# Pre-split first weights kept in DRAM, pairwise sums of the attention weights, and moved steps, in an attention, MLP and expert-MLP kernel

## The chip, the cores and the metric

One core of a Trainium2 chip runs the whole kernel in one launch. The metric is device time in microseconds, median of several runs; lower is better. Engines: PE (TensorE), ACT (ScalarE), DVE (VectorE), POOL (GpSimd), and SP (SyncE), whose queue issues nearly all DMAs.

## The reference

```python
# q, k, v: (4, 12, 448, 64) float32; g_q, g_k: (64,)
q_n, k_n = rmsnorm(q, g_q), rmsnorm(k, g_k)
attn = softmax(q_n @ k_n.T / sqrt(64))          # sum + 1e-9 below the line
x = (attn @ v) laid out as (1792, 768)
h = x @ w_in                                    # (768, 2048), float64 in DRAM
x = (h * clip(h + 3, 0, 6) / 6) @ w_out         # (2048, 768), float64 in DRAM
# then: logits = x @ w_gate (8 experts); greedy assignment by descending logit,
# 224 tokens an expert; out = relu(x @ w1[e]) @ w2[e]
```

All else is float32. The two float64 weights come in as int64 bits.

## The kernel before

Products that must be near float32 are done in fp32r with each operand split in two: a rounded high part `h` (ACT) and a low part `l` = raw - h (DVE or POOL), and three products hh, hl, lh. Attention goes over 24 pairs of heads. One pair takes 16 steps of a schedule of events written out by hand: `at(t, fn, ...)` with t = 16 i + an offset (the T_ constants), sorted by t, gives one program order, which each engine and SP's queue then keep. Pair i's maxima (`s1`, L301/L304, `mt`/`mr` L310/L312) come before its transposed scores (`sT`, L323), the exponentials (L334) and the product with v (`pv`, L413). For 17 of 24 pairs the result stays transposed (head dim by tokens); the other seven (`QMAJOR`: batch 0 and the last pair) go over `av`, `normalize`, `xt`.

For the 17 pairs the sums of the exponentials are made so: POOL adds the four key blocks of each head, three additions in a row (`padd`, L406); PE multiplies with ones (`psums`, L421) and ACT copies it (L423); SP writes two rows to DRAM and reads them back spread over 112 partitions (`rs_out` L427, `rs_in` L432); DVE adds 1e-9 (L436) and inverts (L437); SP writes that out and reads it as a broadcast (`r_out` L441, `r_in` L447); POOL multiplies (`xmul` L452), and ACT and DVE split the result (L460, L461).

Between the steps a queue of atoms is drained by `fill`: the first product of the batch before (`mlp1_atoms`, L499), 16 units of 18 products a batch, for batches 0 to 2. A unit loads its 384 KB of w_in (`win_load`, L174), splits it (`win_split`, ACT L114; DVE or POOL by turns, L115), and ends with the gate (ACT L502, DVE L504) and the store of g (SP, L505). Batch 2 also carries `wprime_atoms`, which fold the router's weights into w_out. Batch 3 follows after attention. The float64 weights are turned into float32 by `conv` and `narrow`: 16 units of 128 columns of w_in from step 20, one every 10 steps, and 16 of w_out from step 180, one every 12; four DVE steps (L137 to L140) on following schedule steps, and a store (L165, L167). All SBUF tiles and the eight PSUM buffers (one ring, tag "b") have a fixed number of buffers.

After attention come batch 3's first product, the second product with the routing between (L1103), and the experts (L1187, L1251); w_out and the experts' weights are loaded and split as units too (`wout_unit`, `moe_unit`).

Of the kernel before, what the change touches and what calls it, by code (L numbers as in the profile page):

```python
# [21 lines left out]
def kernel(  # L22
# [28 lines left out]
    VB, CB = 6, 1  # L51
# [24 lines left out]
    T_ADD, T_PV, T_SUM = (6, 12.5, 14), (17, 17.1, 19.5, 19.6), 21  # L76
    T_RS, T_RL, T_REC, T_RO, T_RB, T_X, T_XS = 24, 26, 30, 31.5, 33, 37, 38.5
# [56 lines left out]
    def narrow(lo, hi, v):  # L134

        vi = v.bitcast(I32)
        return (lambda: nc.vector.tensor_scalar(v, hi.bitcast(F32), 2.0 ** -112, None, op0=OP.mult),  # L137
                lambda: nc.vector.tensor_scalar(vi, vi, 3, None, op0=OP.logical_shift_left),
                lambda: nc.vector.scalar_tensor_tensor(vi, lo, 29, vi, op0=OP.logical_shift_right, op1=OP.bitwise_or),
                lambda: nc.vector.scalar_tensor_tensor(vi, hi, -2147483648, vi, op0=OP.bitwise_and, op1=OP.bitwise_or))  # L140

    RAW = {}

    def conv(key, part):
# [16 lines left out]
        v32, steps = RAW[key]  # L161
        steps[part]()
        if part == 3:
            if out_:
                nc.sync.dma_start(wo32[rows, :], v32)  # L165
            else:
                nc.sync.dma_start(w32[:, rows].rearrange("(c p) f -> p c f", p=128), v32.rearrange("p (c f) -> p c f", c=NC))  # L167
# [9 lines left out]
    def win_split(u, v32):  # L177
        h = wpool.tile([128, NC, 128], F32R, name="wh", tag="w", bufs=WB)
        l = wpool.tile([128, NC, 128], F32R, name="wl", tag="w", bufs=WB)
        split(v32, h, l, nc.vector if u % 2 else nc.gpsimd)  # L180
        return h, l
# [157 lines left out]
    def av(i, s, n):  # L339
# [26 lines left out]
        if (s, n) == (0, QT - 1):  # L366
            NUM[i] = (apool.tile([CP, NCH, 2, D], F32, name="num", bufs=1), apool.tile([CP, 2, NCH], F32, name="scol", bufs=1),
                      apool.tile([CP, NCH, 2, D], F32, name="xq", bufs=1))
# [31 lines left out]
    PA, PV, RC = {}, {}, {}  # L400

    def padd(i, n):
        for s in range(2):
            if n == 1:
                PA[i, s] = apool.tile([CP, S], F32, name="pa", bufs=2)
            nc.gpsimd.tensor_tensor(PA[i, s], PA[i, s] if n > 1 else PP[i, s, 0][0], PP[i, s, n][0], op=OP.add)  # L406
# [11 lines left out]
    def psums(i):  # L418
        p = ps.tile([128, 512], F32, name="sm", tag="b", bufs=8)
        for s, r in enumerate(ROWS):  # L420
            nc.tensor.matmul(p[r, :S], ones64, PA.pop((i, s)), start=True, stop=True)  # L421
        RC[i] = apool.tile([128, S], F32, name="sms", bufs=1)
        nc.scalar.activation(RC[i], p[:, :S], AF.Copy)  # L423

    def rs_out(i):
        d = dram.tile([2, S], F32, name=f"sum_dr{i}")
        nc.sync.dma_start(d, RC[i][0:128:64, :])  # L427
        RC[i] = d
# [6 lines left out]
    def rec(i):  # L435
        nc.vector.tensor_scalar(RC[i], RC[i], eps[:CP], None, op0=OP.add)  # L436
        nc.vector.reciprocal(RC[i], RC[i])  # L437
# [6 lines left out]
    def r_in(i):  # L444
        t = apool.tile([128, S], F32, name="rb", bufs=1)
        for s, r in enumerate(ROWS):
            nc.sync.dma_start(t[r, :], RC[i][s:s + 1, :].to_broadcast([64, S]))  # L447
        RC[i] = t

    def xmul(i):  # L450
        n = PV[i]
        nc.gpsimd.tensor_tensor(n, n, RC.pop(i), op=OP.mult)  # L452

    def xsplit(i):
        b, j = divmod(i, NP)
        if j == 0:
            XT[b] = [xpools[b % 2].tile([128, NC, S], F32R, name=n) for n in ("xh", "xl")]
        xh, xl = XT[b]
        n = PV.pop(i)
        nc.scalar.activation(xh[:, j], n, AF.Copy)  # L460
        nc.vector.tensor_tensor(xl[:, j], n, xh[:, j].bitcast(F32), op=OP.subtract)  # L461
# [4 lines left out]
    units_in = list(range(NF)) * B  # L466
    GB = 2

    def prefetch(splits=2):

        while len(ready) < splits and loaded:
# [4 lines left out]
    def mlp1_atoms(b, inline):  # L476
# [13 lines left out]
        def mm(f, n):  # L490
# [9 lines left out]
            if n == 3 * NC - 1:  # L500
# [4 lines left out]
                nc.sync.dma_start(g_dr[b][f * 128:(f + 1) * 128, :], g)  # L505
                if inline:
                    gsplit(b, f, g, nc.vector)

        for f in range(NF):
            for n in range(3 * NC):  # L510
                atoms.append(lambda f=f, n=n: mm(f, n))
                if inline and n == 10 and f > 1:
                    atoms.append(lambda f=f: lg(b, f - 2))
        if inline:
# [188 lines left out]
    for i in range(NH // 2):  # L703
# [24 lines left out]
        else:  # L728
            for n in range(1, NCH):
                at(t + T_ADD[n - 1], padd, i, n)  # L730
            for d, fn in ((T_SUM, psums), (T_RS, rs_out), (T_RL, rs_in), (T_REC, rec), (T_RO, r_out), (T_RB, r_in), (T_X, xmul), (T_XS, xsplit)):
                at(t + d, fn, i)
        if (i + 1) % NP == 0:
# [4 lines left out]
    for u in range(NF if wide else 0):  # L738
        for out_, t in ((0, T_CI + D_CI * u), (1, T_CO + D_CO * u)):
            at(t - T_CL, conv, (out_, u), -1)  # L740
            for part in range(4):
                at(t + part, conv, (out_, u), part)
# [310 lines left out]
    def moe_tile(name):  # L1053
        k = nw[0] % (WB + EB)
        nw[0] += 1
        if k < WB:
            return wpool.tile([128, 768], F32R, name=name, tag="w", bufs=WB)
        return big_tile(name)

    def moe_unit(e, j, eng, after=None):  # L1060
# [10 lines left out]
        h, l = moe_tile("weh"), moe_tile("wel")  # L1071
# [227 lines left out]
```

## Time and profile before

| what | value |
|---|---|
| median of 3 runs | 1279.39 us (1275.06 to 1279.78) |
| the profiled execution's own time | 1273.12 us |
| its span | 1271.3 us |
| mean granted TensorE clock | 0.962 |
| PE / PEld busy | 1160.6 / 929.6 us |
| DVE / ACT / POOL busy | 861.0 / 549.2 / 559.2 us |
| DMA | 205.68 MB, 162 GB/s |

Times are us from the span's start. PEld is PE's weight load. In a row, `out<-in` names the tiles, x gives the count; "idle before" is time in which the engine stood still just before such an instruction, and `<-` what ended it. The granted clock is the mean over a stretch, as a part of 2.4 GHz. A busy matmul's end is modelled.

### The profile page before, as it was taken

How to read it: one execution, taken by the hardware profiler on the slowest of the kernel's cores; microseconds unless marked ns; L12 is line 12 of the kernel's file. 1: busy time of each engine (PE TensorE's matmuls, PEld its weight loads, DVE VectorE, ACT ScalarE, POOL GpSimd, SP SyncE). 2: the span in 40 equal slices, each digit the busy share in tenths (PEclk: the TensorE clock that was granted, in tenths of full speed). 3: DMA queues.
4: the chain of work that ended last, by engine and by line, in shares of the span. 5: the costliest groups of instructions: out<-in, count | busy, mean ns of one | idle time of the engine just before them, and what ended most of it. 6: DMA issues, size and time to landing. Idle time of an engine off the chain costs nothing.

```text
span 1271.3 us, 19668 instructions
## 1 busy us (share of the span) xinstructions
PE 1160.6 (91%) x7136; PEld 929.6 (73%) x7136; DVE 861.0 (68%) x1662; ACT 549.2 (43%) x1019; POOL 559.2 (44%) x395
## 2 busy tenths in 40 slices
PE   4988798889998998899998999999999799999997
PEld 2877456565655666568776777777777799999997
DVE  7988967878887985444687366666667566655550
ACT  3544454444543544454675311111112565566650
POOL 2212755665766564122344222222224476666641
PEclk9988898999998999999998999999999899999999
DMA  4456666465655555434998422222224888777731
GB/s 126 142 158 182 179 169 178 150 197 156 190 176 168 166 175 165 142 105 127 311 303 269 126 72 63 75 63 76 63 76 108 221 247 246 236 238 235 227 122 44
DMA packets 228885, 205.68 MB, mean 162 GB/s; under 512 B 24082, under 2 KB 208052, under 8 KB 228788
## 3 DMA queue, kind: packets, MB, share of 16 engines
q1 hardware_dynamic: 225460, 193.42, 51.5%
q0 software_dynamic: 3328, 11.01, 2.9%
q8 instruction: 56, 0.92, 0.3%
q14 instruction: 41, 0.34, 0.1%
HBM read 165.99 MB, written 38.39 MB: 161 GB/s over the span
## 4 chain that ended last, share of the span: by engine, by line
PE 38%; DVE 6%; issue 4%; DMA 3%; ACT 1%; POOL 1%; POOLq 0%; DVEq 0%; ACTq 0%
PE y L1103 16%; PE y L1251 8%; PE h L1187 5%; PE h L499 2%; PE h L1189 2%; PE rt L914 2%; DMA we_s<-in_moe_w_dram 1%; DVE C L909 1%; DMA gr<-g_dr 1%; DVE gl L529 1%; PE lg L542 1%; PE lg L541 1%; PE xp L1135 1%; DVE wel L115 1%; ACT weh L114 0%
## 5 line engine op out<-in xcount | busy, mean ns | idle before, releaser
L1047 POOL TENSOR_TENSOR g2l<-gr,g2h 128x512 fp32r<-128x512 f32 x60 | 78.8, 1316 | 210.1 <-ACT g2h L1045 162.8
L499 PE MATMUL h<-xh,wh 128*128 128x448 f32 x384 | 157.3, 410 | 8.6 <-DVE mr L312 4.2
L499 PE MATMUL h<-xl,wh 128*128 128x448 f32 x384 | 147.6, 384 | 0.0
L499 PE MATMUL h<-xh,wl 128*128 128x448 f32 x384 | 147.3, 384 | 0.0
L115 POOL TENSOR_TENSOR wel<-we_s,weh 128x768 fp32r<-128x768 f32 x60 | 119.3, 1994 | 63.2 <-ACT weh L114 52.9
L115 DVE TENSOR_TENSOR wel<-we_s,weh 128x768 fp32r<-128x768 f32 x68 | 93.7, 1385 | 71.4 <-ACT weh L114 71.2
L114 ACT ACTIVATE weh<-we_s 128x768 fp32r<-128x768 f32 x128 | 105.4, 841 | 63.7 <-DMA we_s<-in_moe_w_dram 48.0
L1103 PE MATMUL y<-woh,g2l 128*128 128x512 f32 (+1 forms) x448 | 128.7, 349 | 1.0 <-POOL g2l L1047 1.0
L1187 PE MATMUL h<-xe,weh 128*128 128x448 f32 x384 | 124.6, 385 | 5.3 <-DVE xe L1138 5.3
L1045 ACT ACTIVATE g2h<-gr 128x512 fp32r<-128x512 f32 x60 | 37.7, 631 | 209.3 <-PE y L1103 156.6
L1103 PE MATMUL y<-woh,g2h 128*128 128x512 f32 (+1 forms) x448 | 128.1, 349 | 0.0
L1103 PE MATMUL y<-wol,g2h 128*128 128x512 f32 (+1 forms) x448 | 126.6, 346 | 0.0
L499 PEld LDWEIGHTS h<-xh,wh 128*128 128x128 f32 x384 | 76.0, 198 | 50.9 <-issue 29.7
L334 ACT ACTIVATE ph<-st 112x448 f32<-112x448 f32 x192 | 92.1, 543 | 45.3 <-PE st L323 44.4
L304 DVE TENSOR_REDUCE mx<-s 112x1 f32<-112x448 f32 x192 | 107.0, 611 | 1.3 <-PE s L301 1.2
L115 POOL TENSOR_TENSOR wl<-win_v,wh 128x768 fp32r<-128x768 f32 x32 | 64.0, 2002 | 97.9 <-ACT wh L114 95.8
L406 POOL TENSOR_TENSOR pa<-pa,ph 112x448 f32<-112x448 f32 x68 | 94.4, 1415 | 0.4 <-ACT ph L334 0.4
L1189 PE MATMUL h<-xe,wel 128*128 128x224 f32 x384 | 94.6, 273 | 0.0
L1251 PE MATMUL y<-weh,hl 128*112 128x384 f32 x256 | 86.4, 338 | 0.0
L1251 PE MATMUL y<-weh,hh 128*112 128x384 f32 x256 | 86.3, 337 | 0.0
L1251 PE MATMUL y<-wel,hh 128*112 128x384 f32 x256 | 86.3, 337 | 0.0
L499 PEld LDWEIGHTS h<-xh,wl 128*128 128x128 f32 x384 | 76.1, 198 | 12.5 <-issue 4.1
(249 smaller groups left out, 2664.0 us busy)
## 6 DMA issues: line engine op xcount, KB each, us to landing
we_s<-in_moe_w_dram SPq DMA_DIRECT2D x128, 384.0 KB, 4.5
win_v<-w SPq DMA_DIRECT2D x64, 384.0 KB, 5.0
g_dr<-g SPq DMA_DIRECT2D x64, 224.0 KB, 2.6
gr<-g_dr SPq DMA_DIRECT2D x52, 256.0 KB, 2.9
wraw<-in_moe_w_in_dram SPq DMA_DIRECT2D x16, 768.0 KB, 7.2
wraw<-in_moe_w_out_dram SPq DMA_DIRECT2D x16, 768.0 KB, 6.1
gr<-g_dr SPq DMA_DIRECT2D x48, 224.0 KB, 5.4
w<-cv SPq DMA_DIRECT2D x16, 384.0 KB, 3.1
```

The source lines that it names most:

```text
L114: nc.scalar.activation(hi, raw, AF.Copy)
L115: eng.tensor_tensor(lo, raw, hi.bitcast(F32), op=OP.subtract)
L304: mx = nc.vector.tensor_reduce(MX[i][:, s, c:c + 1], pp[s][:CP, :S], axis=AX.X, op=OP.max)
L334: nc.scalar.activation(e, pp[s][:CP, :S], AF.Exp)
L406: nc.gpsimd.tensor_tensor(PA[i, s], PA[i, s] if n > 1 else PP[i, s, 0][0], PP[i, s, n][0], op=OP.add)
L499: nc.tensor.matmul(p[:, :S], w[:, c], x[:, c], start=(n == 0), stop=(n == 3 * NC - 1))
L1045: nc.scalar.activation(gh, g, AF.Copy)
L1047: eng.tensor_tensor(gl, g, gh.bitcast(F32), op=OP.subtract)
L1103: nc.tensor.matmul(pp[hf][:, :COLS[hf].stop - COLS[hf].start], a[:, f % QF], w[:, COLS[hf]], start=(f == 0 and n == 0), stop=(f == NF - 1 ...
L1187: mm = [lambda: nc.tensor.matmul(p[:, :4 * CP], wh[:, fo], x.rearrange("d k t -> d (k t)"), start=(c == 0), stop=(c == NC - 1), skip_group ...
L1189: lambda: nc.tensor.matmul(p[:, :2 * CP], wl[:, fo], x[:, 0], start=False, stop=False, skip_group_check=True)]
L1251: nc.tensor.matmul(p[:CP, :HW], a[:, f, tk], w[:, o], start=(f == 0 and n == 0), stop=(f == FB - 1 and n == 2))
```

## The change

In `conv`, a unit of w_in is also split right after its conversion (ACT, then POOL), and both parts go to a DRAM tensor `w_hl`. The first 48 units of the first product (batches 0 to 2) load that pair ready made, 768 KB in one transfer (`win_whole`); the last 16 still load float32 and split. The first narrowing step runs on ACT; the store of the converted unit is one step later. `padd` makes two independent additions a head, and `psums` adds their results on PE, four products. The 1e-9 is added by ACT's copy, into the buffer `rb` that then takes the broadcast as well. The places of the chain of the sums move ahead, and `xsplit`'s low part goes to POOL. g is stored six products into the next unit. `normalize` works in place; the stage buffers `v` go from 6 to 4; high and low weight tiles share one buffer each pair.

```diff
     NF = FF // 128
     NTC = NT // 128
     NSL = NT // CP
-    VB, CB = 6, 1
+    VB, CB = 4, 1
     WB = 6
     OB = 3
     PB = 12
...
     T_ST = (0, 0.1, 8, 8.1)
     T_AV = ((17, 18, 19.5, 20.5), (22, 23, 24.5, 25.5))
     T_NUM, T_XT, T_MLP = 28, 33, (37, 41, 41, 37)
-    T_ADD, T_PV, T_SUM = (6, 12.5, 14), (17, 17.1, 19.5, 19.6), 21
-    T_RS, T_RL, T_REC, T_RO, T_RB, T_X, T_XS = 24, 26, 30, 31.5, 33, 37, 38.5
+    T_ADD, T_PV, T_SUM = (6, 14), (17, 17.1, 19.5, 19.6), 21
+    T_RS, T_RL, T_REC, T_RO, T_RB, T_X, T_XH, T_XL = 22.5, 24.5, 27.5, 28.5, 30.5, 35, 36, 37.5
+    GD = 6
     QMAJOR = tuple(range(NP)) + (B * NP - 1,)
     T_CI, D_CI, T_CO, D_CO, T_CL = 20, 10, 180, 12, 14
...
     def narrow(lo, hi, v):
         vi = v.bitcast(I32)
-        return (lambda: nc.vector.tensor_scalar(v, hi.bitcast(F32), 2.0 ** -112, None, op0=OP.mult),
+        return (lambda: nc.scalar.activation(v, hi.bitcast(F32), AF.Copy, scale=2.0 ** -112),
                 lambda: nc.vector.tensor_scalar(vi, vi, 3, None, op0=OP.logical_shift_left),
                 lambda: nc.vector.scalar_tensor_tensor(vi, lo, 29, vi, op0=OP.logical_shift_right, op1=OP.bitwise_or),
                 lambda: nc.vector.scalar_tensor_tensor(vi, hi, -2147483648, vi, op0=OP.bitwise_and, op1=OP.bitwise_or))
     RAW = {}
+    wide_b = range(B - 1) if wide else ()
+    w_hl = [dram.tile([128, 2, 768], F32, name=f"w_hl{u}") for u in range(NF if wide else 0)]
     def conv(key, part):
...
             raw = RAW[key]
             v32 = rawp.tile([128, 768], F32, name="cv", bufs=CB)
             RAW[key] = (v32, narrow(raw[:, :, 0], raw[:, :, 1], v32))
-        v32, steps = RAW[key]
-        steps[part]()
-        if part == 3:
+        v32, steps = RAW[key][:2]
+        if part < 4:
+            steps[part]()
+        elif part == 5:
+            hl = rawp.tile([128, 2, 768], F32R, name="whl", bufs=1)
+            RAW[key] += (hl,)
+            nc.scalar.activation(hl[:, 0], v32, AF.Copy)
+        elif part == 6:
+            hl = RAW[key][2]
+            nc.gpsimd.tensor_tensor(hl[:, 1], v32, hl[:, 0].bitcast(F32), op=OP.subtract)
+        elif part == 8:
+            nc.sync.dma_start(w_hl[n], RAW[key][2].bitcast(F32))
+        elif part == 4:
             if out_:
                 nc.sync.dma_start(wo32[rows, :], v32)
             else:
...
         return u, v32
     def win_split(u, v32):
-        h = wpool.tile([128, NC, 128], F32R, name="wh", tag="w", bufs=WB)
-        l = wpool.tile([128, NC, 128], F32R, name="wl", tag="w", bufs=WB)
-        split(v32, h, l, nc.vector if u % 2 else nc.gpsimd)
-        return h, l
+        w = wpool.tile([128, 2, NC, 128], F32R, name="w", bufs=WB // 2)
+        split(v32, w[:, 0], w[:, 1], nc.vector if u % 2 else nc.gpsimd)
+        return w[:, 0], w[:, 1]
+
+    def win_whole(u):
+        w = wpool.tile([128, 2, NC, 128], F32R, name="w", bufs=WB // 2)
+        nc.sync.dma_start(w.rearrange("p a c f -> p a (c f)").bitcast(F32), w_hl[u])
+        return w[:, 0], w[:, 1]
     a_stack = ExitStack()
...
         if n % QT < QT - 1:
             return
         if (s, n) == (0, QT - 1):
-            NUM[i] = (apool.tile([CP, NCH, 2, D], F32, name="num", bufs=1), apool.tile([CP, 2, NCH], F32, name="scol", bufs=1),
-                      apool.tile([CP, NCH, 2, D], F32, name="xq", bufs=1))
+            NUM[i] = (apool.tile([CP, NCH, 2, D], F32, name="num", bufs=1), apool.tile([CP, 2, NCH], F32, name="scol", bufs=1))
+            NUM[i] += (NUM[i][0],)
         num, sc, _ = NUM[i]
         m = slice(n - QT + 1, n + 1)
         pv = p[:CP, :QT * W].rearrange("p (n w) -> p n w", w=W)
...
         nc.vector.tensor_tensor(xl[:, j], t[:, :S], xh[:, j].bitcast(F32), op=OP.subtract)
-    PA, PV, RC = {}, {}, {}
+    PA, PV, RC, RB = {}, {}, {}, {}
     def padd(i, n):
         for s in range(2):
-            if n == 1:
-                PA[i, s] = apool.tile([CP, S], F32, name="pa", bufs=2)
-            nc.gpsimd.tensor_tensor(PA[i, s], PA[i, s] if n > 1 else PP[i, s, 0][0], PP[i, s, n][0], op=OP.add)
+            PA[i, s, n] = apool.tile([CP, S], F32, name="pa", bufs=4)
+            nc.gpsimd.tensor_tensor(PA[i, s, n], PP[i, s, 2 * n][0], PP[i, s, 2 * n + 1][0], op=OP.add)
     def pv(i, c):
         if c == 0:
...
     def psums(i):
         p = ps.tile([128, 512], F32, name="sm", tag="b", bufs=8)
-        for s, r in enumerate(ROWS):
-            nc.tensor.matmul(p[r, :S], ones64, PA.pop((i, s)), start=True, stop=True)
-        RC[i] = apool.tile([128, S], F32, name="sms", bufs=1)
-        nc.scalar.activation(RC[i], p[:, :S], AF.Copy)
+        for n in range(2):
+            for s, r in enumerate(ROWS):
+                nc.tensor.matmul(p[r, :S], ones64, PA.pop((i, s, n)), start=(n == 0), stop=(n == 1))
+        RB[i] = apool.tile([128, S], F32, name="rb", bufs=1)
+        nc.scalar.activation(RB[i], p[:, :S], AF.Identity, bias=eps)
     def rs_out(i):
         d = dram.tile([2, S], F32, name=f"sum_dr{i}")
-        nc.sync.dma_start(d, RC[i][0:128:64, :])
+        nc.sync.dma_start(d, RB[i][0:128:64, :])
         RC[i] = d
     def rs_in(i):
...
         RC[i] = t
     def rec(i):
-        nc.vector.tensor_scalar(RC[i], RC[i], eps[:CP], None, op0=OP.add)
         nc.vector.reciprocal(RC[i], RC[i])
     def r_out(i):
...
         RC[i] = d
     def r_in(i):
-        t = apool.tile([128, S], F32, name="rb", bufs=1)
+        d = RC.pop(i)
         for s, r in enumerate(ROWS):
-            nc.sync.dma_start(t[r, :], RC[i][s:s + 1, :].to_broadcast([64, S]))
-        RC[i] = t
+            nc.sync.dma_start(RB[i][r, :], d[s:s + 1, :].to_broadcast([64, S]))
     def xmul(i):
         n = PV[i]
-        nc.gpsimd.tensor_tensor(n, n, RC.pop(i), op=OP.mult)
-
-    def xsplit(i):
+        nc.gpsimd.tensor_tensor(n, n, RB.pop(i), op=OP.mult)
+
+    def xsplit(i, lo):
         b, j = divmod(i, NP)
-        if j == 0:
+        if not lo and j == 0:
             XT[b] = [xpools[b % 2].tile([128, NC, S], F32R, name=n) for n in ("xh", "xl")]
         xh, xl = XT[b]
-        n = PV.pop(i)
-        nc.scalar.activation(xh[:, j], n, AF.Copy)
-        nc.vector.tensor_tensor(xl[:, j], n, xh[:, j].bitcast(F32), op=OP.subtract)
+        if lo:
+            nc.gpsimd.tensor_tensor(xl[:, j], PV.pop(i), xh[:, j].bitcast(F32), op=OP.subtract)
+        else:
+            nc.scalar.activation(xh[:, j], PV[i], AF.Copy)
     lgp = {}
     late, tpool, ready, loaded = [], [], [], []
     units_in = list(range(NF)) * B
+    whole = [len(wide_b) * NF]
     GB = 2
     def prefetch(splits=2):
+        while whole[0] and len(ready) < splits:
+            ready.append(win_whole(units_in.pop(0)))
+            whole[0] -= 1
+        if whole[0]:
+            return
         while len(ready) < splits and loaded:
             ready.append(win_split(*loaded.pop(0)))
         while units_in and len(loaded) < 3 and (len(units_in) > NF or len(loaded) + len(ready) < 3 or tpool):
...
                 nc.scalar.activation(r, p[:, :S], AF.Relu, bias=half, scale=1.0 / 6.0)
                 g = mpool.tile([128, S], F32, name="g", bufs=GB)
                 nc.vector.scalar_tensor_tensor(g, r, 1.0, p[:, :S], op0=OP.min, op1=OP.mult)
-                nc.sync.dma_start(g_dr[b][f * 128:(f + 1) * 128, :], g)
+                state["g", f] = g
                 if inline:
                     gsplit(b, f, g, nc.vector)
+
+        def g_out(f):
+            nc.sync.dma_start(g_dr[b][f * 128:(f + 1) * 128, :], state.pop(("g", f)))
         for f in range(NF):
             for n in range(3 * NC):
                 atoms.append(lambda f=f, n=n: mm(f, n))
+                if n == GD and f > 0:
+                    atoms.append(lambda f=f: g_out(f - 1))
                 if inline and n == 10 and f > 1:
                     atoms.append(lambda f=f: lg(b, f - 2))
+        atoms.append(lambda: g_out(NF - 1))
         if inline:
             for f in (NF - 2, NF - 1):
                 late.append(lambda f=f: lg(b, f))
...
             at(t + T_NUM, normalize, i)
             at(t + T_XT, xt, i)
         else:
-            for n in range(1, NCH):
-                at(t + T_ADD[n - 1], padd, i, n)
-            for d, fn in ((T_SUM, psums), (T_RS, rs_out), (T_RL, rs_in), (T_REC, rec), (T_RO, r_out), (T_RB, r_in), (T_X, xmul), (T_XS, xsplit)):
+            for n in range(2):
+                at(t + T_ADD[n], padd, i, n)
+            for d, fn in ((T_SUM, psums), (T_RS, rs_out), (T_RL, rs_in), (T_REC, rec), (T_RO, r_out), (T_RB, r_in), (T_X, xmul)):
                 at(t + d, fn, i)
+            at(t + T_XH, xsplit, i, False)
+            at(t + T_XL, xsplit, i, True)
         if (i + 1) % NP == 0:
             at(t + T_MLP[i // NP], mlp_next, i // NP)
     at(T_LOAD, load_scales)
...
     for u in range(NF if wide else 0):
         for out_, t in ((0, T_CI + D_CI * u), (1, T_CO + D_CO * u)):
             at(t - T_CL, conv, (out_, u), -1)
-            for part in range(4):
-                at(t + part, conv, (out_, u), part)
+            for part in range(5 if out_ else 9):
+                if part != 7:
+                    at(t + part, conv, (out_, u), part)
     events.sort(key=lambda e: e[:2])
     ENDS = [8 * H * (b + 1) - 16 + T_MLP[b] for b in range(B)]
     now = 0
...
```

## Rows read from the trace of the kernel before

**Rows 1.** Windows: stretch, length, busy PE, PEld, DVE, ACT, POOL; clock, DMA share, GB/s

```profile
50.00:150.00 100.00, 84.08 (x667) 68.36 (x664) 88.98 (x170) 49.22 (x100) 34.43 (x28) 0.91 0.67 182
150.00:300.00 150.00, 132.45 (x692) 87.23 (x690) 120.43 (x186) 71.00 (x128) 87.44 (x61) 0.94 0.58 170
300.00:450.00 150.00, 137.98 (x725) 93.61 (x726) 126.59 (x195) 71.40 (x131) 92.25 (x63) 0.94 0.57 177
450.00:570.00 120.00, 106.42 (x601) 72.59 (x600) 64.09 (x113) 54.08 (x120) 47.69 (x36) 0.94 0.47 145
570.00:690.00 120.00, 110.29 (x584) 89.33 (x583) 86.63 (x124) 74.94 (x137) 46.20 (x29) 0.97 0.83 257
```

**Rows 2.** Waits of PE, 150 to 570: us in total, times, longest

```profile
PE t L278 <- DVE mx L304: 6.2, 2, 3.5
...
PE s L301 <- DVE g L504: 0.4, 1, 0.4
```

**Rows 3.** Lines: busy us, mean ns, idle before and its releasers

```profile
L115 DVE TENSOR_TENSOR wl<-win_v,wh 128x768 fp32r<-128x768 f32 x32 | 40.2, 1255 | 3.4 <-ACT wh L114 2.0 <-PE lg L541 1.0
...
L115 POOL TENSOR_TENSOR wl<-win_v,wh 128x768 fp32r<-128x768 f32 x32 | 64.0, 2002 | 97.9 <-ACT wh L114 95.8 <-DMA ld_q<-in_q_dram 2.1
...
L114 ACT ACTIVATE wh<-win_v 128x768 fp32r<-128x768 f32 x64 | 53.7, 840 | 4.2 <-DMA win_v<-w 2.1 <-issue 1.1 <-PE h L499 1.0
...
L137 DVE TENSOR_SCALAR cv<-wraw 128x768 f32<-128x768 f32 x32 | 24.2, 757 | 0.7 <-DMA w<-cv 0.7
...
L461 DVE TENSOR_TENSOR xl<-xn_t,xh 128x448 fp32r<-128x448 f32 x17 | 16.5, 970 | 26.8 <-ACT xh L460 26.8
...
L436 DVE TENSOR_SCALAR rs<-rs,eps 112x8 f32<-112x8 f32 x17 | 13.4, 786 | 28.0 <-DMA rs<-sum_dr 28.0
...
L406 POOL TENSOR_TENSOR pa<-pa,ph 112x448 f32<-112x448 f32 x68 | 94.4, 1415 | 0.4 <-ACT ph L334 0.4
...
L406 POOL TENSOR_TENSOR pa<-ph 112x448 f32<-112x448 f32 x34 | 43.8, 1307 | 3.3 <-PE sm L421 2.3 <-ACT ph L334 0.9
...
L421 PE MATMUL sm<-pa,ones 112*64 112x448 f32 x68 | 16.5, 564 | 1.4 <-DVE mx L304 1.4
...
L452 POOL TENSOR_TENSOR xn_t<-xn_t,rb 128x448 f32<-128x448 f32 x17 | 21.3, 1253 | 123.1 <-DMA rb<-rec_dr 100.2 <-PE st L323 16.4 <-DVE scol L378 6.5
...
L240 ACT ACT_TABLE_LOAD x1 | 1.3, 1283 | 0.7 <-PEq L1283 0.7
```

**Rows 4.** Lines, DVE alone, 50 to 150

```profile
L137 DVE TENSOR_SCALAR cv<-wraw 128x768 f32<-128x768 f32 x10 | 8.1, 806 | 0.7 <-DMA w<-cv 0.7
...
L138 DVE TENSOR_SCALAR cv<-cv 128x768 int32<-128x768 int32 x9 | 7.3, 806 | 0.2
```

**Rows 5.** Instructions of line 138: ns min/median/max

```profile
L138 DVE TENSOR_SCALAR cv<-cv x32: 546/554/2095, 42.0 to 544.1; 128x768 int32<-128x768 int32 x32
```

**Rows 6.** DMA issues: count, KB each, us to landing

```profile
win_v<-w SPq DMA_DIRECT2D x64, 384.0 KB, 5.0
...
wraw<-in_moe_w_in_dram SPq DMA_DIRECT2D x16, 768.0 KB, 7.2
```

**Rows 7.** Waits of SP's queue, 0 to 600

```profile
SPq L505 <- DVE g L504: 95.0, 26, 10.1
SPq L167 <- DVE cv L140: 79.3, 13, 13.9
```

**Rows 8.** Timeline, 290 to 323: start us, us

```profile
293.55 0.55 ACT L423 ACTIVATE sms<-sm 128x448 f32<-128x448 f32 x1 [0.72 <-PE sm L421]
...
300.89 0.50 SPq L427 DMA_DIRECT2D sum_dr<-sms  x1
...
317.66 0.55 ACT L423 ACTIVATE sms<-sm 128x448 f32<-128x448 f32 x1
...
319.73 1.47 POOL L452 TENSOR_TENSOR xn_t<-xn_t,rb 128x448 f32<-128x448 f32 x1
```

More of the change, by code (lines that the diff above doesn't have):

```diff
@@ L1051, with moe_tiles @@
     nw = [0]
-    def moe_tile(name):
-        k = nw[0] % (WB + EB)
+    def moe_tiles():
+        k = nw[0] % ((WB + EB) // 2)
         nw[0] += 1
-        if k < WB:
-            return wpool.tile([128, 768], F32R, name=name, tag="w", bufs=WB)
-        return big_tile(name)
+        if k < WB // 2:
+            w = wpool.tile([128, 2, 768], F32R, name="w", bufs=WB // 2)
+            return w[:, 0], w[:, 1]
+        return big_tile("weh"), big_tile("wel")
     def moe_unit(e, j, eng, after=None):
@@ L1070, in moe_unit @@
                               reason="the gather goes first")
-        h, l = moe_tile("weh"), moe_tile("wel")
+        h, l = moe_tiles()
         split(v32, h, l, eng or (nc.vector if j % 2 else nc.gpsimd))
```

## The prediction

> **What bounds the kernel now.** I read the busy time by stretch first. The edits lie in the first 570 us: attention, with the first product of batches 0 to 2 between its steps. From 50 to 150 us, where mostly attention and the conversion of w_in run, VectorE is busy 89.0 of 100 us and TensorE waits for it. From 150 to 570 TensorE is ahead: 132.45 + 137.98 + 106.42 = 376.9 busy of 420 us, VectorE 311.1, ScalarE 196.5, GpSimd 227.4 [rows 1]. Two losses are to be seen there: TensorE stands still for 43.1 us, and its granted clock is 0.94. The two levels are 1.2 and 2.4 GHz, so 0.94 means 2 x 0.06 = 12% of the time, 50 us, at the lower one; at a busy share of 0.90 about 22 us of work time are lost to it.
>
> Second, what TensorE stood still for: eleven rows of that stretch name VectorE, 38.1 us in all, of which the first and the last stand here; three name ScalarE with 4.4 us [rows 2]. VectorE is not full from 150 on, but it works in order, and it also stands still itself: 28.0 us for the sums that come back from DRAM (L436) and 26.8 us for ScalarE's rounding of x (L461) [rows 3]. So a product that TensorE wants is late because VectorE is held by, or busy with, something less urgent. After 570 us the third batch's remainder, batch 3 and everything else run as before.
>
> **The change part by part.** The sum is made against the profiled execution's own 1273.12 us (span 1271.3); the median of the three runs is 1279.39, 6.3 above it, and I add that at the end.
>
> *VectorE from 150 to 570.* 48 of 64 splits of w_in go; half were VectorE's: 24 x 1.255 = 30.1 us. The first narrowing step goes to ScalarE: of its 32, 22 lie here, 22 x 0.757 = 16.7. The low part of x goes to GpSimd: 16.5. The addition of eps goes into ScalarE's copy: 13.4 [rows 3]. Together 76.7 us of 311.1, so VectorE falls to 234 of 420, 56%. The wait of 26.8 for the rounding leaves it too; that of 28.0 passes to the reciprocal. I take it that two thirds of TensorE's 38.1 us behind VectorE go: -25. Low clock follows standing still here (its stretches lie among these waits), so of the 22 us I take half: -11. From both sides: nothing goes, or all 43 + 22 = 65.
>
> *Four products for the sums.* TensorE does a second pair of products per head pair, 17 pairs. The 68 records have a mean of 564 ns, 38.4 us laid end to end, but only 16.5 busy, as the two heads run side by side [rows 3]. I add as much again: +16.5; were they to run one after the other, 38.4. It lies on TensorE, so no cover is assumed. What is late next is ScalarE's copy of the sums, by 1 us.
>
> *ScalarE.* -48 x 0.840 = -40.3 (roundings of w_in), +32 narrowing steps, +16 roundings for the stored pair, 13.4. No such narrowing step is seen on ScalarE (every second word, times a constant). I take the 0.840 of a rounding of the same 768 columns, 26.9, so the balance is 0. The bounds: VectorE did the step in 0.757, 24 us in all; its longest single instruction of this shape among the three others is near 2.5 times a rounding [rows 3, 5], 67 us, which ScalarE, busy 246 of 520 us [rows 1], holds at a cost of perhaps a tenth on TensorE, 4 us. Adding eps as a bias uses a function that the trace before does not have. The single table load took 1.283 us [rows 3]; if it needed its own table, two loads a pair would be 34 x 1.283 = 43.6 us on ScalarE; I take 0. *Trainium skill, "ScalarE: Activation LUTs", section "Table sets: the hidden batching unit": cheap functions, identity among them, are filler in every set; by that no load is added. Copy, square, exp and relu ran on one load in this trace, which agrees; no run here shows identity.*
>
> *GpSimd.* -24 x 2.002 (splits), -34 additions at about 1.36 (102 before at 94.4 + 43.8 us, 68 after), +16 x 2.002 (low part of the stored pair), +17 x 1.253 (low part of x, priced as the multiplication of the same shape): -48.0 - 46.2 + 32.0 + 21.3 = -41 us [rows 3]. It is not on TensorE's path: 0.
>
> *50 to 150 us.* Ten narrowing steps leave VectorE, 10 x 0.806 = 8.1 [rows 4]. Against it nine subtractions of 2.0 us come to GpSimd, at 34.4 busy. VectorE is slower when GpSimd works: the shift L138 took 0.806 on average in this stretch [rows 4] where its median is 0.554 and its longest 2.095 [rows 5]. With 18 us more GpSimd and some 5 less, that excess of 0.25 rises to about 0.35; for three steps of nine units +3. Net -5, one for one, as VectorE is full there; bounds -9 and +10 (every new subtraction holds it for its whole 2.0 us).
>
> *The rule behind the excess.* *Trainium skill, "SBUF — State Buffer", section "SBUF: two separate sides": VectorE and GpSimd share a port pair that is locked for a whole instruction, and the loser fully blocks. The longest L138, 2.095 = 0.55 + 1.5, looks like that, its median does not. By the rule alone the stretch would lose ten us; that is a rival below.*
>
> *Loads.* Each of 48 loads grows from 384 to 768 KB and 16 stores of 768 KB come: 18.9 + 12.6 = 31.5 MB over 520 us, 61 GB/s on 145 to 182. In 570:690 the queues moved 257 [rows 1], so there is room. Landing goes from 5.0 to the 7.2 us of a load of that size [rows 6]; it is issued two units ahead, and with 420 / 48 = 8.75 us a unit that is 17 us of cover: 0. If the cover went (the buffer free one unit late), 7.2 us against 8.75 would still fit. SP now stands at each unit's start until TensorE is through with the unit before, since that frees the buffer; queued behind it are the small transfers of the sums and the loads of later pairs. Before, it stood at the same place longer: 95.0 us for VectorE's gate (L505), and 79.3 for the fourth narrowing step (L167) [rows 7]. Both stores now come later (six products into the next unit; one step later), which frees SP for what is behind. I count 0, and use it for the rivals. The stage buffers fall from 6 to 4, and no unit before the 49th uses them: 0.
>
> *Earlier steps for the sums.* All places of the chain move ahead by 1.5 to 3 steps of some 1.5 us. The copy of the sums, the broadcast and the product share one buffer now, so ScalarE's copy for a pair waits until GpSimd's multiplication of the pair before is done. Before, one pair shows the copy at 317.66 and the earlier pair's multiplication at 319.73 for 1.47 [rows 8]: 3.5 us too late. This repeats for 16 pairs, from 1.8 early to 6.7 late, mean 2.4. With two steps, 3 us, gained, seven pairs would still be late, 12 us together on ScalarE; SP's lost time comes back to this chain too (the copy of 293.55 left at 300.89 [rows 8], 7 us later, because SP stood at a gate store). I take 0, bounds 0 and +41.
>
> Sum: -25 - 11 + 16.5 - 5 = -24.5; 1273.1 - 24.5 = 1248.6 on the profile's footing, 1255 as a median. After 570 us nothing: those loads and splits are the old ones.
>
> **The rivals.** *ScalarE stops at the shared buffer (slower).* It decides from the point where the multiplication ends after the next pair's copy is due. If the chain does not move up although its places do (SP is in order, and its waits for TensorE hold it), 16 x 2.4 + the late tail = 41 us on ScalarE, all handed to TensorE through the exponentials queued behind: 1248.6 + 41 = 1290, median 1296. For it: the lateness seen; GpSimd stood 100.2 us for that broadcast [rows 3]. Against it: SP loses its longest waits. Chance 0.13.
>
> *The waits change their name.* VectorE is relieved but TensorE waits for the exponentials instead; a third of the losses goes, -13 - 7: with +16.5 and -5 that is -8 at best, and 0 if the earlier stretch gives nothing. 1269, median 1275. For it: GpSimd and VectorE were not full after 150. Against it: only 4.4 us were ScalarE's. Chance 0.17.
>
> *The port lock.* 50:150 loses 10 instead of gaining 5: 1264, median 1270. Chance 0.07.
>
> *All of it.* Standing still and low clock vanish: -65 + 16.5 - 5 = -53, median 1226. Against it: a transposition that waits for the last reduction of maxima before it (L310) will still wait. Chance 0.08.
>
> **How the numbers follow.** The forecast holds 0.55, with 1240 to 1269 as its own range. Half a per cent, 6 us, is what a measurement of this kernel tells from no change. Faster by more (below 1273): 0.53 of the forecast, the lock's 0.05, all of the eighth, 0.06 of the renamed waits: 0.72. Within: 0.11 of the renamed waits, 0.02 each of forecast and lock: 0.15. Slower: the shared buffer's 0.13. The range of 8 in 10 runs from 1230 to 1284: below lies half of the "all" case, above most of the slower one.
>
> **What would show it.** Right: VectorE near 235 of the same work, TensorE's rows behind VectorE under 15 us, granted clock 0.96 or more before 550, the sums' product at 33 us busy, the end of attention some 25 us earlier, and an unchanged length behind it. Wrong: rows in which ScalarE's copy of the sums waits for GpSimd's multiplication, rows in which VectorE's reciprocal waits longer than 28 us for the sums, a table load a pair, or TensorE waiting for a whole unit's load.

## The result, and the profile after

The changed kernel takes 1238.64 us (1236.28 to 1239.39), the kernel before 1277.22 in the same comparison: ratio 0.9704, 95% interval 0.9658 to 0.975. Forecast were 1255 and a range of 1230 to 1284. The span fell from 1271.3 to 1237.1 us.

The windows after, columns as in [rows 1]:

```profile
50.00:150.00 100.00, 90.83 (x640) 77.19 (x637) 77.50 (x144) 58.22 (x110) 37.20 (x29) 0.79 0.72 229
150.00:300.00 150.00, 138.83 (x759) 91.79 (x758) 99.89 (x179) 73.81 (x133) 76.59 (x61) 0.97 0.81 263
300.00:450.00 150.00, 145.79 (x811) 97.20 (x810) 94.61 (x170) 72.53 (x133) 60.90 (x51) 0.98 0.73 236
450.00:570.00 120.00, 119.46 (x748) 89.96 (x746) 55.86 (x113) 58.17 (x134) 30.82 (x25) 1.00 0.60 205
570.00:690.00 120.00, 109.18 (x532) 85.87 (x533) 87.83 (x114) 70.28 (x124) 45.37 (x29) 0.96 0.85 262
```

Against [rows 1]: from 150 to 570 TensorE is busy 404.1 of 420 us instead of 376.9, at 0.97 to 1.00 of its clock instead of 0.94, and VectorE 250.4 instead of 311.1. From 50 to 150 it is the other way: the clock is 0.79 instead of 0.91. Fixed windows hold different work in the two kernels, so I also cut by events: the starts of VectorE's `mr` of pairs 2, 8, 12, 20 and 23 (L312; after, L329), of its gate of the last unit of batches 2 and 3, and the end. Lengths in us:

| stretch | before | after | moved |
|---|---|---|---|
| start to pair 2 | 45.7 | 44.9 | -0.8 |
| pair 2 to 8 ("A") | 101.7 | 109.5 | +7.8 |
| pair 8 to 12 | 105.2 | 99.3 | -5.9 |
| pair 12 to 20 | 190.1 | 176.3 | -13.8 |
| pair 20 to 23 | 96.2 | 76.2 | -20.0 |
| pair 23 to end of batch 2 | 59.8 | 60.0 | +0.2 |
| batch 3 | 91.6 | 95.2 | +3.6 |
| rest | 581.0 | 575.6 | -5.4 |

Pair 8 to the end of batch 2 ("B") holds the gain: 451.4 to 411.8, -39.6. The rest is between 575 and 581 us in all the profiles of this document, in no order that the edits explain, so I read nothing from that row. Over the two stretches B, between these cuts, the windows are (before, then after):

```profile
147.40:598.80 451.40, 407.60 (x2216) 280.50 (x2217) 326.42 (x526) 210.35 (x409) 236.22 (x164) 0.94 0.54 162
154.40:566.30 411.90, 397.07 (x2272) 273.55 (x2273) 243.61 (x447) 200.89 (x392) 163.88 (x132) 0.98 0.72 236
```

TensorE's waits from 150 to 570 after the change, all that are left; eleven rows of VectorE with 38.1 us [rows 2] have become two with 12.6:

```profile
PE s L318 <- DVE mr L329: 8.0, 6, 2.8
PE s L318 <- DVE g L526: 4.6, 3, 2.4
PE s L318 <- ACT ph L351: 2.9, 2, 2.7
```

The groups after that answer to [rows 3]:

```profile
L422 POOL TENSOR_TENSOR pa<-ph 112x448 f32<-112x448 f32 x68 | 84.6, 1265 | 15.7 <-ACT ph L351 11.6 <-PE sm L438 4.0
...
L438 PE MATMUL sm<-pa,ones 112*64 112x448 f32 x136 | 29.3, 552 | 0.0
L173 POOL TENSOR_TENSOR whl<-cv,whl 128x768 fp32r<-128x768 f32 x16 | 29.3, 1831 | 65.4 <-ACT whl L170 52.3 <-DVE st L265 9.4 <-issue 3.6
L138 ACT ACTIVATE cv<-wraw 128x768 f32<-128x768 f32 x32 | 28.7, 898 | 2.6 <-POOL whl L173 1.3 <-DMA w<-cv 1.1
...
L475 POOL TENSOR_TENSOR xl<-xn_t,xh 128x448 fp32r<-128x448 f32 x17 | 19.5, 1147 | 34.1 <-ACT xh L477 34.1
...
L440 ACT ACTIVATE rb<-sm,eps 128x448 f32<-128x448 f32 x17 | 10.8, 636 | 13.9 <-PE sm L438 13.9
...
L453 DVE RECIPROCAL rs<-rs 112x8 f32<-112x8 f32 x17 | 3.3, 197 | 17.5 <-DMA rs<-sum_dr 17.5
...
L257 ACT ACT_TABLE_LOAD x1 | 1.3, 1283 | 0.7 <-PEq L1315 0.7
```

The sums' copy (L440) waits for the product alone, not for GpSimd; the reciprocal waits 17.5 us where the addition before it waited 28.0; there is one table load; the products for the sums went from 16.5 to 29.3 us. TensorE waits for no whole load. So none of the prediction's signs of being wrong appeared; of its signs of being right the clock failed from 50 to 150 us. SP's queue, against [rows 7]:

```profile
SPq L180 <- DVE cv L141: 58.1, 9, 13.3
SPq L197 <- PE h L521: 50.5, 20, 6.7
...
SPq L532 <- DVE g L526: 19.9, 7, 5.1
```

The gate holds SP 19.9 instead of 95.0 us; the whole loads (L197) now hold it for TensorE, 50.5; the conversion's stores (L180) hold it for VectorE, 58.1.

### The profile page after: what moved, and what is told of

It reads as the page before. It is cut to its first block, busy times and chain, and to the rows that moved or that the text cites. A ratio compares the mean times of both kernels' runs of the same rounds, so it can differ in the third digit from the quotient of the medians.

```text
span 1237.1 us, 19781 instructions
## 1 busy us (share of the span) xinstructions
PE 1159.3 (94%) x7204; PEld 933.1 (75%) x7204; DVE 777.0 (63%) x1572; ACT 553.6 (45%) x1019; POOL 500.7 (40%) x370
## 4 chain that ended last, share of the span: by engine, by line
PE 66%; DVE 15%; DMA 8%; issue 6%; ACT 3%; POOL 1%; SPq 0%; POOLq 0%; DVEq 0%; ACTq 0%
PE y L1135 16%; PE h L521 14%; PE y L1283 8%; PE h L1219 5%; PE st L340 4%; PE av L380 4%; PE av L429 3%; PE h L1221 3%; DMA rec_dr<-rs 2%; DVE mx L321 2%; PE rt L945 2%; DVE cv L140 1%; DMA rb<-rec_dr 1%; DMA wo_s<-wo 1%; PE s L318 1%
## 5 line engine op out<-in xcount | busy, mean ns | idle before, releaser
L521 PE MATMUL h<-xh,w 128*128 128x448 f32 x768 | 244.1, 385 | 0.0
L521 PEld LDWEIGHTS h<-xh,w 128*128 128x128 f32 x768 | 145.0, 193 | 42.6 <-issue 27.1
L1078 POOL TENSOR_TENSOR g2l<-gr,g2h 128x512 fp32r<-128x512 f32 x60 | 79.7, 1329 | 205.5 <-ACT g2h L1076 159.6
L521 PE MATMUL h<-xl,w 128*128 128x448 f32 x384 | 148.4, 386 | 0.0
L116 POOL TENSOR_TENSOR wel<-we_s,weh 128x768 fp32r<-128x768 f32 x48 | 98.1, 2047 | 41.9 <-ACT weh L115 32.4
L1219 PE MATMUL h<-xe,weh 128*128 128x448 f32 x318 | 100.3, 375 | 0.5 <-DVE xe L1170 0.5
L521 PEld LDWEIGHTS h<-xl,w 128*128 128x128 f32 x384 | 74.0, 193 | 22.5 <-issue 16.3
L422 POOL TENSOR_TENSOR pa<-ph 112x448 f32<-112x448 f32 x68 | 84.6, 1265 | 15.7 <-ACT ph L351 11.6
L1135 PEld LDWEIGHTS y<-woh,g2l 128*128 128x128 f32 x448 | 72.8, 189 | 11.0 <-POOL g2l L1078 1.3
L1135 PEld LDWEIGHTS y<-woh,g2h 128*128 128x128 f32 x448 | 72.5, 189 | 10.4 <-issue 1.3
L1135 PEld LDWEIGHTS y<-wol,g2h 128*128 128x128 f32 x448 | 72.5, 189 | 9.7
```

Source lines behind the costliest of these rows:

```text
L116: eng.tensor_tensor(lo, raw, hi.bitcast(F32), op=OP.subtract)
L422: nc.gpsimd.tensor_tensor(PA[i, s, n], PP[i, s, 2 * n][0], PP[i, s, 2 * n + 1][0], op=OP.add)
L521: nc.tensor.matmul(p[:, :S], w[:, c], x[:, c], start=(n == 0), stop=(n == 3 * NC - 1))
L1078: eng.tensor_tensor(gl, g, gh.bitcast(F32), op=OP.subtract)
L1135: nc.tensor.matmul(pp[hf][:, :COLS[hf].stop - COLS[hf].start], a[:, f % QF], w[:, COLS[hf]], start=(f == 0 and n == 0), stop=(f == NF - 1 ...
L1219: mm = [lambda: nc.tensor.matmul(p[:, :4 * CP], wh[:, fo], x.rearrange("d k t -> d (k t)"), start=(c == 0), stop=(c == NC - 1), skip_group ...
```

## The experiments

Ratios are against the kernel before as measured beside each kernel (its medians there: 1273.9 to 1277.5 us), with 95% intervals, so between groups of runs the ratios compare better than the medians. A and B are read from one profile each. "Low" is the time at the lower clock level in A. In the diffs `...` marks lines left out.

| kernel | median | ratio | A | low in A | B |
|---|---|---|---|---|---|
| before | 1277.22 | 1 | 101.7 | 17.2 | 451.4 |
| after | 1238.64 | 0.9704 (0.9658 to 0.975) | 109.5 | 44.4 | 411.8 |
| e1 | 1257.44 | 0.9861 (0.9816 to 0.9905) | 108.4 | 37.5 | 424.8 |
| e2 | 1236.84 | 0.9684 (0.9648 to 0.972) | 99.7 | 20.5 | 411.0 |
| e3 | 1243.0 | 0.9726 (0.9688 to 0.9764) | 107.3 | 34.1 | 411.7 |
| e4 | 1236.55 | 0.9681 (0.9647 to 0.9715) | 109.5 | 44.4 | 408.1 |
| e5 | 1251.2 | 0.9811 (0.9776 to 0.9846) | 107.4 | 41.0 | 423.2 |
| e6 | 1240.55 | 0.9744 (0.9703 to 0.9784) | 108.2 | 34.1 | 412.7 |
| e7 | 1247.26 | 0.9786 (0.9749 to 0.9823) | 117.4 | 58.0 | 409.6 |
| e8 | 1279.55 | 1.0044 (1.002 to 1.0068) | 101.7 | 17.2 | 453.7 |
| e9 | 1264.83 | 0.9928 (0.9899 to 0.9957) | 129.4 | 61.4 | 412.5 |
| e10 | 1243.15 | 0.9772 (0.971 to 0.9834) | 108.6 | 44.4 | 415.0 |
| e11 | 1251.35 | 0.9821 (0.9778 to 0.9865) | 103.1 | 27.3 | 425.8 |
| e12 | 1254.04 | 0.9835 (0.9792 to 0.9879) | 103.0 | 23.9 | 428.8 |

**e1, the stored pair alone** (the change's `conv` parts 5 to 8, `win_whole`, `prefetch`, VB = 4, put into the kernel before, with the shared weight tiles).

> The kernel before with one part of the change alone: w_in split once, kept as a pair, loaded whole for three batches (stage buffers 6 to 4 with it). Theory V (what leaves VectorE after 150 us is what TensorE gains): the pair takes 30.1 of the 76.7 us that the whole change takes off VectorE there, so 40% of a gross gain of some 49 us, -19 us, and the first stretch loses up to 5: 1258 to 1264 us against 1277. Theory S (SP's later stores and the earlier chain of the sums made the gain): no change, 1273 to 1281.

Measured 1257, about what theory V had, A 6.7 us longer included. The pair also takes work off ScalarE and GpSimd (in B 26 and 46 us less busy), so this gain alone does not show that VectorE's relief makes it.

**e2, the pair undone.**

```diff
-    VB, CB = 4, 1
+    VB, CB = 6, 1
...
-    wide_b = range(B - 1) if wide else ()
+    wide_b = ()
...
-            for part in range(5 if out_ else 9):
+            for part in range(5):
```

> The changed kernel with that part alone undone (float32 loads and splits for all 64 units, stage buffers back to 6). Theory V: it loses what the pair alone gains, 1239 + 19 = 1254 to 1260 us; but the first stretch (first pairs to 160 us) is some 5 us shorter again. Theory S: within 5 us of the changed kernel, 1236 to 1244.

Measured 1237: not slower than the changed kernel, the intervals overlap. Theory V fails as a sum: what gains 20 us alone is worth nothing beside the rest. A is 9.8 us shorter, B as long; in this profile batch 3 and the rest are 3 and 5 us longer, which is why the total hardly moves.

**e3, the narrowing step back on VectorE.**

```diff
-        return (lambda: nc.scalar.activation(v, hi.bitcast(F32), AF.Copy, scale=2.0 ** -112),
+        return (lambda: nc.vector.tensor_scalar(v, hi.bitcast(F32), 2.0 ** -112, None, op0=OP.mult),
```

> The changed kernel with the first narrowing step back on VectorE. Theory V: 16.7 us more on VectorE after 150, about half of it shown on TensorE, and 8 us more before 150: 1248 to 1254 us. Rival E (the step on ScalarE makes ScalarE and VectorE wait for each other, and that is why the first stretch, pairs 2 to 8, grew from 101.7 to 109.5 us): that stretch shrinks by 5 to 8 us and the total is 1232 to 1240.

Measured 1243, B unchanged, A 2.2 us shorter: neither theory's range; the step is worth at most a few us and does not explain A.

**e4, three additions and two products again** (`padd` and `psums` as before the change, T_ADD = (6, 12.5, 14)).

> The changed kernel with the old sums: three additions in a row per head on GpSimd, two products. If TensorE is full after 150 us, as its 404 of 420 busy us say, 29.3 - 16.5 = 12.8 us of products go and the time falls nearly as much: 1226 to 1231 us. Rival G (the additions on GpSimd, 41 us more, make the sums late and ScalarE or VectorE wait for them): 1238 to 1248.

Measured 1237, B 3.7 us shorter in its profile: 12.8 us less of products show as 2 us, inside the interval. Neither expectation held. In B TensorE is busy 7.3 us less (389.8) and stands still 3.5 us more (18.3), and GpSimd is busy 41.6 us more (205.5): the edit brings the chained additions back with the products gone, so it does not price the four products by themselves.

**e5, g stored at the end of its unit again.**

```diff
-                state["g", f] = g
+                nc.sync.dma_start(g_dr[b][f * 128:(f + 1) * 128, :], g)
...
-                if n == GD and f > 0:
-                    atoms.append(lambda f=f: g_out(f - 1))
...
-        atoms.append(lambda: g_out(NF - 1))
```

> The changed kernel with g stored at the end of its unit again. The pair undone cost nothing (1237) while the pair alone gained 20, so the parts overlap. Theory S (SP, which no longer stands behind VectorE's gate, brings loads and the sums' transfers in time): SP's wait for the gate returns to some 90 us and the time rises to 1250 to 1258. Theory V (relief of VectorE, from whichever part, is what TensorE gains): 1236 to 1243.

Measured 1251, B 11.4 us longer, and SP stands for the gate again (0 to 600 us):

```profile
SPq L527 <- DVE g L526: 92.2, 27, 6.4
```

That is theory S. But e8 is against it as a whole:

**e8, the later stores alone** (e5's edit the other way round, in the kernel before).

> The kernel before with g stored six products into the next unit, nothing else. Theory S: 1258 to 1264 us against 1277. Theory V: 1273 to 1279.

Measured 1280, no gain and rather a loss, although SP's wait for the gate fell to 40.4 from 95.0 us here too. SP stands for the conversion's last narrowing step instead: for the stores of w_out's units 76.7 us, 51.5 before.

```profile
SPq L165 <- DVE cv L140: 76.7, 13, 10.4
SPq L510 <- DVE g L504: 40.4, 13, 8.1
```

**e6, x's low part back on VectorE** (`nc.gpsimd` to `nc.vector` in `xsplit`).

> The changed kernel with the low part of x back on VectorE (one step earlier in the order than before the change). Theory V: 16.5 us of VectorE come back and with them its wait for ScalarE's rounding (26.8 us before), of which TensorE sees a part: 1245 to 1252. Theory S: 1236 to 1242.

Measured 1241, B 0.9 us longer: theory V's 6 us or more are not there (5 us by the ratios, whose intervals overlap).

**e11, neither the pair nor the later stores** (e2's and e5's edits together).

> The changed kernel without the stored pair and with g stored at once: what is left is the relief of VectorE by 46.6 us (narrowing, low part of x, eps), the two additions and four products, and the moved chain. Stores alone gained nothing (1280), stores undone beside the pair cost 13. Theory O (the waits lie behind each other: SP's standing behind the gate shows only once VectorE is relieved): 1246 to 1254. Theory P (the later stores matter only because the wide loads stand in the same queue): 1235 to 1241.

Measured 1251, theory O. What is left in e11 (the relief, together with the new sums and the moved chain, which no run takes apart) takes B from 451 to 426, the later stores on top of it to 411 (e2); alone they gain nothing (454). TensorE's waits behind VectorE from 150 to 570 go the same way in these four: 38.1 before, 34.8 in e8, 27.7 in e11, 14.7 in e2; after, 12.6. They are not the whole account: e1 has 21.9 and e5 16.5 at a B as long as e11's, and e5 waits 7.9 for ScalarE besides (after, 2.9).

**e7, the pair made two steps later.**

```diff
-                    at(t + part, conv, (out_, u), part)
+                    at(t + {5: 7.0, 6: 8.0, 8: 9.6}.get(part, part), conv, (out_, u), part)
```

> The changed kernel with the three steps that make the stored pair moved from 5, 6 and 8 steps after the unit's start to 7, 8 and 9.6. Theory L (ScalarE stands in order before the pair's rounding until VectorE has finished the fourth narrowing step, 7.9 us in 45:150, holds up attention behind it and lets TensorE's clock fall to 0.79): the wait goes, the stretch from pair 2 to pair 8 falls from 109.5 to 100 to 104 us with the clock back to 0.90, total 1229 to 1234. Rival D (it is the pair's work itself, GpSimd's subtraction against VectorE and 768 KB stores): the stretch stays at 107 to 112, total 1237 to 1241.

Theory L falls: ScalarE's wait before the pair's rounding in A went from 7.9 (first row, the changed kernel) to 0.4 us (last row, e7),

```profile
ACT whl L170 <- DVE cv L141: 7.9, 4, 3.4
...
ACT cv L138 <- POOL whl L173: 3.5, 2, 2.2
...
ACT whl L170 <- DVE cv L141: 0.4, 1, 0.4
```

and A became longer still, 117.4, at a clock of 0.75 (stretch, length, busy PE, PEld, DVE, ACT, POOL; clock):

```profile
45.00:162.00 117.00, 104.10 (x690) 86.75 (x690) 84.12 (x161) 60.97 (x115) 44.45 (x34) 0.75 0.69 216
```

Rival D's ranges, 107 to 112 and 1237 to 1241, were missed too: at 1247 the move cost 9 us, and why is open.

**e9, batch 0 on the transposed path.**

```diff
-    T_NUM, T_XT, T_MLP = 28, 33, (37, 41, 41, 37)
+    T_NUM, T_XT, T_MLP = 28, 33, (41, 41, 41, 37)
...
-    QMAJOR = tuple(range(NP)) + (B * NP - 1,)
+    QMAJOR = (B * NP - 1,)
```

> The changed kernel with the six pairs of batch 0 on the transposed path as well (448-column products with v instead of 66-column ones; the start of batch 0's first product moves from 37 to 41 steps, as for batches 1 and 2). Theory C (from pair 2 to pair 8 the 66-column products run at the lower clock for 44 us and are then the chain; that made this stretch 7.8 us longer): low clock there falls under 20 us, the stretch from 109.5 to 88 to 98 us, total 1222 to 1230. Rival K (the sums' chain, 27 us long for a pair that takes 13 to 17 us here, and one shared buffer hold ScalarE): the stretch is 110 us or more, total 1239 or more.

Measured 1265, rival K. The longest pieces of the chain of waits in A are the transfers of the sums (start, us), 35% of it together:

```profile
52.47 7.23 DMA rec_dr<-rs
90.81 6.91 DMA rs<-sum_dr
115.17 5.43 DMA rec_dr<-rs
141.05 4.61 DMA rb<-rec_dr
157.57 6.45 DMA rec_dr<-rs
```

It tells nothing of the pair, since these transfers are now in the chain.

**e10, the sums' chain at its old places.**

```diff
-    T_RS, T_RL, T_REC, T_RO, T_RB, T_X, T_XH, T_XL = 22.5, 24.5, 27.5, 28.5, 30.5, 35, 36, 37.5
+    T_RS, T_RL, T_REC, T_RO, T_RB, T_X, T_XH, T_XL = 24, 26, 30, 31.5, 33, 37, 38.5, 39
```

> The changed kernel with the places of the sums' chain as before the change (multiplication and next pair's copy of the sums at the same step again), the buffer still shared. Rival of the prediction (ScalarE stops at the shared buffer): ScalarE's copy of the sums waits for GpSimd's multiplication, 20 to 40 us in all, total 1250 to 1275. Theory S (with the stores later, SP brings the chain in time anyway): under 8 us of such waits, total 1237 to 1244.

Measured 1243, 4 us slower by the medians and 9 by the ratios; the intervals overlap. The total is in theory S's range, but its waits are not under 8 us: the wait of the slower rival is there, which the changed kernel does not have (ScalarE, 0 to 600 us):

```profile
ACT rb L440 <- POOL xn_t L467: 11.6, 5, 5.4
```

So the shared buffer holds ScalarE where the chain is late, and the moved places avoid that. The price on TensorE is small: B is 3.2 us longer, and one TensorE wait of 1.8 us names this copy.

**e12, the pair made at first use.** Batch 0 splits as before the change; the pair is stored from the weight buffer. `prefetch` is rewritten for it, and the stage buffers are 6 again.

```diff
+        def pair_out(f):
+            h = state["w"][2]
+            nc.sync.dma_start(w_hl[f], h.rearrange("p a c f -> p a (c f)").bitcast(F32))
...
+                if n == 2 * GD and b == 0 and wide:
+                    atoms.append(lambda f=f: pair_out(f))
```

> The changed kernel with the pair made elsewhere: batch 0 loads float32 and splits as before the change, and each unit's split is stored to DRAM from the weight buffer in the middle of its own products; batches 1 and 2 load it whole. ScalarE's and GpSimd's 16 extra instructions in the conversion are gone (stage buffers back to 6). Theory D (making the pair in the conversion is what lengthens the first stretch, and loading it whole is what shortens pairs 20 to 23): pair 2 to pair 8 takes 98 to 103 us as without the pair, pair 20 to 23 takes 75 to 79 as with it, total 1224 to 1233. Rival Q (the stores and wide loads cost what the splits saved): 1236 to 1242.

Both halves of theory D came: A is 103.0, pairs 20 to 23 take 78.8. The total did not: pairs 8 to 12 take 113.8 instead of 99.3, and there the next split waits until the store has read the weight buffer (ScalarE, 149 to 262 us):

```profile
ACT w L115 <- DMA w_hl<-w: 31.3, 8, 8.6
```

No version beats the changed kernel clearly; e2 and e4 are level with it.

## Why the prediction was right, and where its sum was not

B was forecast at -25 - 11 + 16.5 = -19.5 us and gained 39.6. The direction, the place and the kind of the gain were right: TensorE stood behind VectorE, two thirds of that went (38.1 to 12.6 us, -25.5; forecast -25), and the low clock went with it (in B from 51.0 to 17.1 us). By the two windows of B, TensorE stands still 29.0 us less (43.8 to 14.8), and its busy time, forecast to grow by 16.5 - 11 = 5.5 us, fell by 10.5. ScalarE's new work, the table load, the broadcast's shared buffer and GpSimd cost nothing in B that shows.

The size was partly luck. 1238.64 lies in the outer range, but just below the forecast's own range of 1240 to 1269, between the forecast and the rival "All of it" (1226), and the terms that were off in B were all too pessimistic. Of the 20 us that B gained beyond the sum, 11.4 are the later stores (B of e5 is 423.2); the other 9 lie in the four products and the low clock (34 us less at half the clock are some 15 to 17 us of work, an estimate; forecast 11), not told apart. On the other side A and batch 3 grew by 11 us in all, where the sum had -5 and 0. Term by term:

*Four products, +16.5.* They are 12.8 us more busy time, but undoing them (e4) moves the total by 2 and B by 3.7. The forecast charged TensorE's time one for one, some 13 us too much, as far as e4 shows it: it gives GpSimd the chained additions back as well.

*Later stores, 0.* They are worth 13 to 15 us: 1239 against 1251 (e5), 1237 against 1251 (e11); 14 to 17 by the ratios. The step "I count 0" failed. Alone they are worth nothing (e8). The two orders of undoing show that the waits lie behind one another. What they lie behind can be read from VectorE's wait for the sums on their way through DRAM (0 to 600 us; the changed kernel, e2, e5, e11, e8):

```profile
DVE rs L453 <- DMA rs<-sum_dr: 17.5, 6, 6.8
DVE rs L453 <- DMA rs<-sum_dr: 18.2, 5, 6.6
DVE rs L453 <- DMA rs<-sum_dr: 31.3, 7, 9.2
DVE rs L453 <- DMA rs<-sum_dr: 31.7, 8, 6.1
DVE rs L436 <- DMA rs<-sum_dr: 25.8, 7, 8.0
```

It is shorter in all kernels with later stores and relief (11.6 to 22.2) and long in the two that lack the later stores. In e8 it stays near the 28.0 of the kernel before, where SP stands for the narrowing instead. The longest wait of TensorE in B of e5 can be followed back to it: VectorE stands for the sums, ScalarE in order behind VectorE's narrowing, TensorE behind the exponentials that come next on ScalarE:

```profile
241.78 0.20 DVE L453 RECIPROCAL rs<-rs 112x8 f32<-112x8 f32 x1 [6.42 <-DMA rs<-sum_dr]
243.84 0.84 ACT L170 ACTIVATE whl<-cv 128x768 fp32r<-128x768 f32 x1 [9.53 <-DVE cv L141]
245.17 0.71 PE L318 MATMUL s<-kh,qh 64*112 64x448 f32 x1 [7.46 <-ACT ph L351]
```

So the sums' transfers are among those that come too late; that they are the only ones is not shown.

*50 to 150 us, -5.* A grew by 7.8, and the pair is the cause: every kernel that makes it in the conversion has an A of 107 or more, and the kernels that do not and keep batch 0's path 99.7 to 103.1. It is the making and not the whole loads: the first of those is issued at 141 us, after the low stretches shown below. The form of the loss is the lower clock. Against e2, TensorE does the same 690 products in A, is busy 11.7 us longer and stands still 2.7 us less (e2, then the changed kernel):

```profile
45.00:145.00 100.00, 87.08 (x690) 70.53 (x690) 85.24 (x165) 55.18 (x107) 30.26 (x26) 0.90 0.68 183
45.00:154.00 109.00, 98.76 (x690) 83.48 (x690) 85.34 (x160) 61.41 (x115) 44.73 (x34) 0.80 0.71 226
```

Over all kernels but e9, A goes with the time at the lower level: 17.2 us go with 101.7, 58.0 with 117.4, 0.38 us longer for each us at half speed. In the changed kernel the lower level holds for three stretches of 13.7 us in which TensorE is busy nearly all the time, each after one at the higher level in which it was not. Two of them:

```profile
60.00:67.70 7.70, 5.31 (x49) 4.33 (x46) 5.93 (x12) 5.81 (x13) 4.16 (x4) 1.00 1.02 310
67.70:81.40 13.70, 13.70 (x75) 12.55 (x74) 11.54 (x25) 6.55 (x13) 2.56 (x2) 0.50 0.52 171
81.40:101.80 20.40, 18.03 (x167) 15.64 (x166) 16.42 (x31) 13.37 (x26) 9.01 (x8) 1.00 0.77 245
101.80:115.50 13.70, 13.70 (x74) 12.38 (x74) 12.22 (x27) 7.59 (x15) 3.88 (x3) 0.50 0.72 226
```

The prediction had the low clock follow standing still; here it outlasts it. In the chain of waits of 45 to 154 us, 24 products with v take 4.41 us after the change,

```profile
73.08 4.41 PE av L380 x24
106.43 4.41 PE av L380 x24
```

and 2.32 in e2:

```profile
55.41 2.32 PE av L380 x24
```

Why making the pair keeps the clock low stays open. ScalarE's wait is not it (e7), and the port lock of the rival is not either: VectorE's busy time, in which a held instruction counts, fell in A from 90.0 to 85.3 us, as forecast, and is 85.2 in e2 without the pair, where the lock would have raised it. GpSimd's and ScalarE's share and the 768 KB stores were not tried apart.

*The pair.* 30 of the 76.7 us that VectorE was to lose were its splits; theory V of e1 let them count in proportion. It is worth 20 us alone (e1) and nothing beside the rest (e2): with the rest of the relief and the later stores, B is at 411 already, and 408 to 415 in all kernels that keep these two, except e12 (428.8). Loading it whole still shortens pairs 20 to 23 (76.2 against 84.5 in e2), and making it gives that back in A and pairs 8 to 12 (99.3 against 91.7).

*Batch 3, 0.* It grew by 3.6 us. In e8, which has the weight tiles apart like the kernel before, it takes 91.1; in all the others, where high and low share one buffer, 94.1 to 98.4. That buffer is all that e1 and e2 have in common; no run undid it alone.

## What to carry to other kernels

Parts that relieve the same wait do not add: a part that is worth 20 us alone can be worth nothing in the bundle, and one that is worth nothing alone can be worth 13 behind another, so undo each from the finished kernel as well as trying it alone. On an in-order DMA queue, ask of each store what it makes the queue wait for, and put it where its data is long done. Work added on other engines can cost through the tensor engine's clock: here its busy time for the same products grew by 11.7 us while its waits did not. Read the granted clock by stretch.

## What the hardware did that was not expected

From 150 to 570 us the queues moved 205 to 263 instead of 145 to 177 GB/s, and the small transfers of the sums took longer to land: the median of `rs<-sum_dr` (3.5 KB) went from 1.8 to 4.4 us, of `rec_dr<-rs` from 4.1 to 5.2. The rate alone does not explain it: `rs<-sum_dr` has 2.1 in e10 at 209 to 261 GB/s and 3.3 in e8 at 140 to 175. What else does is open.

The excess of VectorE's shift L138 in the kernel before goes with GpSimd one instruction at a time: 17 of the 32 ran beside no GpSimd instruction and took 0.546 to 0.561 us, 15 ran beside one, and ten of these took 1.321 to 2.095.

On ScalarE the narrowing step, which reads every second word, took 0.898 us where a rounding of as many columns took 0.840, and the copy with a bias held in a tile 0.636 where the plain copy took 0.546.
